# Attention and mixture-of-depths on one core: v's split parts stored once, by batch and chunk of 18 tokens, and fetched by an indirect gather

## The chip, the cores and the metric

The kernel runs on one core of a Trainium2 chip, as a single launch. The metric is the device time of that core in microseconds; the time given is the median of three executions, and one further execution was taken with the hardware profiler. Five engines work side by side, each through its own instructions in a fixed order: PE (matrix products), DVE (vector work), ACT (scalar functions), POOL and SP. SP and POOL also start the transfers (DMAs) between the device memory and the on-chip memory.

## What is computed

There are 8 batches, 8 heads, 576 tokens, head size 64 and 32 memory slots. Softmax weights of phi compress k and v into 32 memory slots for each head, each query attends to those slots, and a mixture-of-depths layer then adds a gated feed-forward result to the 128 tokens of highest score in each batch.

```
a = exp(phi - max(phi));  a = a / (sum(a) + 1e-9)          # over the 32 slots
k_m = einsum('bhsm,bhsd->bhmd', a, k)
v_m = einsum('bhsm,bhsd->bhmd', a, v)
scores = (q @ k_m^T) / 8;  attn = softmax(scores)
x = (attn @ v_m) as (batch, token, 8*64)
s = x @ w_gate;  top = the 128 tokens of largest s in each batch
out = x;  out[top] = x[top] + sigmoid(s[top]) * (relu(x[top] @ w1) @ w2)
```

## The kernel before

**Softmax.** The 8 heads of a batch are two groups of 4, so there are 16 pairs (batch, group). `chain_of` is the softmax of one pair on a tile of 128 partitions x 576 tokens. It is a chain of about twenty DVE passes (L332 to L401) and some ACT passes, and two chains run interleaved. `keys` then turns the result with PE transposes (L425), splits it into a high and a low part on ACT (`ahi`, L433) and DVE (`alo`, L435), sums k_m, and sends both parts to device memory as `a_lanes` (`store_a`, L474).

**Splitting v.** `split_v` loads v of a pair, `split` rounds it to a high part on ACT (L501) and takes the rest on DVE (L503), and `store_v` (L484) writes both parts to device memory as `v_lanes`. Each part is written twice, once for each value of `alpha`, since the products need high and low parts of a against high and low parts of v.

**The sum over tokens.** `sums` computes v_m token by token. Four batches (lanes) of 32 partitions each run at once, shifted against one another by LAG chunks. A chunk is T = 16 tokens and takes T x 4 = 64 matmuls (L564). There are 99 chunks. For each chunk `load_rows` fetches one tile of v (`load_v`, L521, one DMA over up to 128 partitions) and eight small tiles of a (`load_a`, L526) into one of three pairs of buffers (`v_rows`, `a_rows`). The memory on the chip is filled with zeros once at the start by POOL (L259), since the a tiles are block-diagonal.

**Attention and feed-forward.** When a batch's 576 tokens are summed, `attention` and `ffn` for it follow on the same engines.

**What sets the order.** The program is written by generators, one for each stream of work, and the class `Plan` decides at build time which step comes next. Each `yield` names an engine, an estimated duration, the buffers that are needed and the size of a transfer. A step with engine "Q" goes to SP or POOL, whichever the plan has free first. The result is a fixed order on each engine: an instruction that waits holds back everything behind it on that engine. Eight transfers can be under way on POOL's queue and eight on SP's, since each issue waits for the one eight places before it.

Of the kernel before, what the change touches and what calls it, by code (L numbers as in the profile page):

```python
# [8 lines left out]
F32 = mybir.dt.float32  # L9
# [3 lines left out]
I32 = mybir.dt.int32  # L13
I16 = mybir.dt.int16
AF = mybir.ActivationFunctionType
ALU = mybir.AluOpType
# [3 lines left out]
P = 128  # L20
# [12 lines left out]
RCP_B, RCP_S, RCP_C = 0.391, 0.70169533, 0.29830515  # L33
GRID, Y0, DH = 2.0 ** -11, 2.0 ** 14, 2.0 ** 9
Y0_BIAS = 14 * 0.6931471805599453
LANES, T, LAG, AHEAD = 4, 16, 9, 9


class Plan:
# [100 lines left out]
def kernel(  # L140
# [7 lines left out]
    w1: bass.AP,  # L148
    w2: bass.AP,
    out: bass.AP,  # L150
    v_lanes: bass.AP,
    a_lanes: bass.AP,
    capacity: int,
):
    nc = tc.nc
# [7 lines left out]
    H = NG * NPR  # L163
# [7 lines left out]
    per = S // T  # L171
    steps = (B - 1) * LAG + per
    assert LANES * LAG >= per
    assert capacity <= P and capacity < S and S % T == 0

    mem = ctx.enter_context(tc.tile_pool(name="mem", bufs=1))
    psum = ctx.enter_context(tc.tile_pool(name="psum", bufs=1, space=PSUM))
# [1 line left out]
    def sb(shape, dtype=F32, name="sb"):  # L179
        return mem.tile(list(shape), dtype, name=name)  # L180

    def several(n, shape, dtype=F32, name="sb"):
        return [sb(shape, dtype, f"{name}{i}") for i in range(n)]
# [11 lines left out]
    means = sb([P, NPR, P], name="means")  # L195
    ones16 = sb([P, P], BF16, name="ones16")
    ones = sb([P, 1], name="ones")
    good = sb([P, B], name="good")
    tgs = several(B, [P, NT, 2], name="tg")
    accs = [psum.tile([P, 512], F32, name=f"acc{i}") for i in range(LANES)]  # L200
# [6 lines left out]
        "ph": several(4, [P, S], name="ph"),  # L207
        "w": several(8, [P, S], name="w"),
        "i": several(2, [P, 2, S], I16, name="i"),
        "big": several(5, [P, S * Dh * NPR // P], name="big"),  # L210
        "vt": ["one", "two"],
        "kb": several(1, [PT, NC, NPR * Dh], name="kb"),
        "aS": several(1, [P, NPR, NC, M], name="aS"),
# [36 lines left out]
    def constants():  # L250
        nc.gpsimd.memset(blocks, 0.0)
        nc.gpsimd.memset(means, 0.0)
        for r in range(NPR):
            p = slice(r * M, (r + 1) * M)
            nc.gpsimd.memset(blocks[p, p], 1.0 / M)
            nc.gpsimd.memset(means[p, r], 1.0 / M)
        for pair in rows:
            for t in pair:
                nc.gpsimd.memset(t.bitcast(F32), 0.0)  # L259
        yield "POOL", 14.0  # L260
        nc.vector.tensor_sub(centre_m, ident, blocks)
        yield "wait", ("a", 0)
        yield "SP", 0.6, (), 256
        nc.sync.dma_start(out=wg, in_=bass.AP(
            tensor=w_gate.tensor, offset=w_gate.offset,
            ap=[[0, P]] + [list(x) for x in w_gate.ap]))
        yield "POOL", 8.0
        nc.gpsimd.iota(iota_r, pattern=[[1, capacity]], base=0, channel_multiplier=0,
                       allow_small_or_imprecise_dtypes=True)
        nc.gpsimd.iota(place, pattern=[[P, NT]], base=0, channel_multiplier=1,  # L270
                       allow_small_or_imprecise_dtypes=True)
        nc.gpsimd.memset(later, 1.0)
        nc.gpsimd.affine_select(
            out=later, in_=later, compare_op=ALU.is_gt, fill=0.0, base=0,
            pattern=[[1, S]], channel_multiplier=-1)
        nc.gpsimd.memset(ones16, 1.0)
        nc.gpsimd.memset(ones, 1.0)
        for t in tgs:
            nc.gpsimd.memset(t, 0.0)
            nc.gpsimd.iota(t[:, :, 0], pattern=[[P, NT]], base=0, channel_multiplier=1,  # L280
                           allow_small_or_imprecise_dtypes=True)
        for t in zs:
            nc.gpsimd.memset(t, 0.0)
            for r in range(NPR):
                nc.gpsimd.memset(t[r * M:(r + 1) * M, :, NPR * Dh + r:NPR * Dh + r + 1], 1.0)
        for t in rds:
            nc.gpsimd.memset(t, 1.0)
        signal("constants")
# [178 lines left out]
    def col(b):  # L467
        return start(b) * T
# [8 lines left out]
        signal(("a", b), 2 * NG)  # L477

    def store_v(b, g, w, src):
        yield "POOL", 1.4, (), 1152  # L480
        for alpha in range(2):
            r0 = ((b % LANES) * 4 + alpha * 2 + w) * H + g * NPR
            dst = v_lanes[r0:r0 + NPR, col(b):col(b) + S]
            nc.gpsimd.dma_start(out=dst.rearrange("h (j s) d -> j h (s d)", j=P // NPR), in_=src)  # L484
        put("big", src)
        signal(("v", b), 2 * NG)

# [20 lines left out]
    def lane(j, g):  # L508
        for b in range(g, B, LANES):
            if 0 <= j - start(b) < per:  # L510
                return b, j - start(b)

    def active(j):
        return [g for g in range(LANES) if lane(j, g)]

    turn = {}

    def load_v(j, eng):
        on = active(j)
        p = slice(32 * on[0], 32 * on[-1] + 32)  # L520
        eng.dma_start(out=turn[j][0].bitcast(F32)[p, :T], in_=v_lanes[p, j * T:(j + 1) * T])  # L521

    def load_a(j, h, eng):
        on = active(j)
# [7 lines left out]
    def load_rows():  # L532
        for j in range(steps):
            on = active(j)
            for g in on:
                b, n = lane(j, g)
                if n == 0:
                    yield "wait", ("v", b)
                    yield "wait", ("a", b)
            q, turn[j] = yield "Q", 0.65, ("rows",), 8 * T * (on[-1] + 1 - on[0])  # L540
            load_v(j, queues[q])
            signal(("rows", j), H + 1)
            for h in range(H):
                q, = yield "Q", 0.6, (), T * (on[-1] + 1 - on[0]) // 2
                load_a(j, h, queues[q])
                signal(("rows", j), H + 1)
# [375 lines left out]
```

## Time and profile before

| | us |
|---|---|
| median of three executions | 734.48 |
| lowest and highest of them | 728.63 and 737.57 |
| the profiled execution, its own time | 731.21 |
| span in its trace, first to last instruction | 729.5 |
| PE busy | 515.3 |
| DVE busy | 445.7 |
| POOL busy | 333.1 |
| ACT busy | 291.7 |

The busy times are sums over the whole span, and the program has stages that are limited by different things, so the table alone doesn't tell what a change in one stage is worth. 165.92 MB were moved, at 227 GB/s on average.

### The profile page before, as it was taken

To read this page: it belongs to the slowest core of one execution; us is meant where nothing else is said; L and a number is where in the kernel's file an instruction comes from. 1 tells how busy PE (TensorE), PEld (TensorE's weight loads), DVE (VectorE), ACT (ScalarE), POOL (GpSimd) and SP (SyncE) were. 2 spreads that over 40 slices of the span, in tenths; PEclk is the share of its full clock that TensorE was granted. 3 is DMA by queue.
4 is the path that set the end of the run, shared out by engine and by line. 5 is a ranking of instruction groups with operands and counts; after the bars stand their busy time and mean duration, and the time that the engine had idled before them with its cause. 6 is when DMAs were issued, how large, how long until landed. Compare 5 with 4: busy or idle time off the path is not lost. (4 is left out here: it accounts for less than half of the span.)

```text
span 729.5 us, 21974 instructions
## 1 busy us (share of the span) xinstructions
PE 515.3 (71%) x8754; PEld 418.8 (57%) x8754; DVE 445.7 (61%) x947; ACT 291.7 (40%) x721; POOL 333.1 (46%) x618
## 2 busy tenths in 40 slices
PE   0021572575776736766787896999999999989991
PEld 0010562465665735555666775678877887747760
DVE  8999987566764999967995222434353342547600
ACT  5466562441532746734663122322222322335310
POOL 9325763656555634554334544365566553010110
PEclk9985686787676757878779899899999999989997
DMA  4999699798889999999999799598865743141200
GB/s 162 384 358 343 168 299 286 201 251 208 215 226 255 362 356 258 318 342 365 284 282 332 235 295 347 179 291 230 226 176 142 175 117 101 37 138 37 66 30 19
DMA packets 74757, 165.92 MB, mean 227 GB/s; under 512 B 22296, under 2 KB 30488, under 8 KB 74648
## 3 DMA queue, kind: packets, MB, share of 16 engines
q0 software_dynamic: 32672, 88.23, 37.6%
q1 hardware_dynamic: 41976, 76.21, 35.5%
q8 instruction: 72, 1.18, 0.7%
q14 instruction: 37, 0.30, 0.1%
HBM read 96.21 MB, written 68.16 MB: 225 GB/s over the span
## 5 line engine op out<-in xcount | busy, mean ns | idle before, releaser
L564 PE MATMUL acc<-a_rows,v_rows 32*128 32x256 f32 x6336 | 253.0, 313 | 93.9 <-DMA a_rows<-a_lanes 63.3
L564 PEld LDWEIGHTS acc<-a_rows,v_rows 32*128 32x128 f32 x6336 | 231.7, 214 | 120.4 <-issue 61.3
L526 POOL DMA_DIRECT2D a_rows<-a_lanes x366 | 186.0, 514 | 122.8 <-PE acc L564 28.0
L706 ACT ACTIVATE w<-bank,rd 128x64 f32<-128x64 f32 (+1 forms) x320 | 69.4, 328 | 84.9 <-DVE rd L701 65.3
L824 PE MATMUL bank<-w,w 128*128 128x128 f32 x512 | 71.5, 292 | 1.0 <-ACT w L813 1.0
L824 PEld LDWEIGHTS bank<-w,w 128*128 128x128 f32 x512 | 65.3, 201 | 9.6 <-issue 4.2
L521 POOL DMA_DIRECT2D v_rows<-v_lanes x52 | 28.3, 545 | 87.3 <-PE acc L564 67.5
L840 PE MATMUL bank<-w,w 128*128 128x512 f32 x128 | 66.1, 622 | 0.0
L425 PE MATMUL bank<-ident,ph 128*96 128x128 f32 x96 | 21.8, 359 | 50.6 <-DVE ph L401 50.6
L693 PE MATMUL bank<-z,w 128*128 128x260 f32 (+1 forms) x160 | 49.2, 436 | 11.4 <-ACT w L654 10.3
L710 DVE TENSOR_TENSOR w<-w,hb 128x512 f32<-128x512 f32 (+1 forms) x40 | 27.5, 688 | 44.6 <-ACT w L706 43.4
L484 POOL DMA_DIRECT2D v_lanes<-big x64 | 35.4, 557 | 33.8 <-ACT big L501 13.3
L246 ACT ACTIVATE w<-i,c 128x576 f32<-128x576 int16 (+1 forms) x48 | 36.4, 766 | 26.1 <-DVE w L362 26.1
L429 ACT ACTIVATE aS<-bank 96x384 f32<-96x384 f32 x32 | 15.4, 486 | 77.2 <-PE bank L425 77.2
L425 PEld LDWEIGHTS bank<-ident,ph 128*96 128x96 f32 x96 | 14.3, 190 | 55.5 <-issue 44.8
L693 PEld LDWEIGHTS bank<-z,w 128*128 128x128 f32 (+1 forms) x160 | 28.7, 199 | 24.2 <-ACT w L654 11.6
L701 DVE RECIPROCAL rd<-bank 128x4 f32<-128x4 f32 (+1 forms) x80 | 11.8, 171 | 45.2 <-PE bank L693 44.9
L435 DVE TENSOR_TENSOR alo<-aS,ahi 96x768 f32<-96x768 f32 x16 | 15.2, 948 | 37.2 <-ACT ahi L433 37.0
L752 DVE SCALAR_TENSOR_TENSOR more<-w,tg,later 128x576 bf16<-128x576 f32 (+4 forms) x40 | 19.7, 546 | 23.9 <-ACT w L742 23.8
L713 DVE TENSOR_TENSOR w<-w,wg 128x512 f32<-128x512 f32 (+1 forms) x40 | 27.4, 686 | 10.4 <-PE bank L693 7.8
L802 POOL DMA_INDIRECT w<-out,idx x8 | 8.9, 1116 | 53.4 <-DVE idx L782 34.9
L474 POOL DMA_DIRECT2D a_lanes<-ahi x32 | 23.1, 724 | 21.8 <-ACT ahi L433 16.5
(118 smaller groups left out, 782.5 us busy)
## 6 DMA issues: line engine op xcount, KB each, us to landing
v_lanes<-big POOLq DMA_DIRECT2D x64, 576.0 KB
v_rows<-v_lanes SPq DMA_DIRECT2D x26, 512.0 KB
v_rows<-v_lanes POOLq DMA_DIRECT2D x19, 512.0 KB
big<-in_v SPq DMA_DIRECT2D x16, 576.0 KB
kb<-in_k SPq DMA_DIRECT2D x16, 576.0 KB
a_lanes<-ahi POOLq DMA_DIRECT2D x32, 288.0 KB
a_lanes<-alo POOLq DMA_DIRECT2D x32, 288.0 KB
big<-in_qT SPq DMA_DIRECT2D x16, 512.0 KB
```

What stands on the lines that cost most here:

```text
L246: nc.scalar.activation(dst, src, func, bias=biases[c] if c else 0.0, scale=s)
L425: nc.tensor.transpose(out=tp[:, c], in_=a[:, c0 + c], identity=ident)
L484: nc.gpsimd.dma_start(out=dst.rearrange("h (j s) d -> j h (s d)", j=P // NPR), in_=src)
L521: eng.dma_start(out=turn[j][0].bitcast(F32)[p, :T], in_=v_lanes[p, j * T:(j + 1) * T])
L526: eng.dma_start(out=turn[j][1].bitcast(F32)[32 * g0 + h:32 * g1:H, h].rearrange("p s m -> p (s m)"), in_=a_lanes[h, 4 * g0:4 * g1, j * T:( ...
L564: nc.tensor.matmul(out=accs[g][:, x * H * M:(x + 1) * H * M].rearrange("p (h m) -> p h m", m=M), lhsT=vr[p, s:s + 2].rearrange("p t d -> p ...
L693: nc.tensor.matmul(out=os[g][:n, :NPR * Dh + NPR], lhsT=e[:, g, t0:t0 + n], rhs=z[:, g], start=True, stop=True)
L706: nc.scalar.activation(x[:n, h * Dh:(h + 1) * Dh], os[g][:n, r * Dh:(r + 1) * Dh], AF.Copy, scale=rd[:n, c, h:h + 1])
L710: nc.vector.tensor_add(x[:n, :D], x[:n, :D], hb[:n].rearrange("p g r d -> p (g r d)"))
L713: nc.vector.tensor_mul(prod[:n, :D], x[:n, :D], wg[:n])
L824: nc.tensor.matmul(out=bank[:, f * P:f * P + n], lhsT=w1s[d, f0 // 4][:, f * P:(f + 1) * P], rhs=xeT[:, d * P:d * P + n], start=(d == 0), ...
L840: nc.tensor.matmul(out=bank[:n], lhsT=hT[f // 4][:, f % 4 * P:f % 4 * P + n], rhs=w2s[f], start=(f == 0), stop=(f == KF - 1))
```

## The change

The two parts of v are stored once. The new tensor `v_rows` in device memory is ordered by batch, chunk and row (16 rows, a part and a head each), and a row holds the 18 tokens of one chunk, 4,608 bytes. So `store_v` issues one DMA where it issued two. T becomes 18, and LAG and AHEAD become 8; a batch has 32 chunks, and there are 88 chunks in all. A chunk still covers 4 lanes, with 72 matmuls. `load_v` becomes an indirect DMA on POOL: for each of up to 128 partitions a row number is read from the on-chip table `v_row`, so that the 16 rows of a batch are each fetched to two partitions. The table is made in `constants()` at the start: POOL clears it and fills it with 32 iotas and one more (`lane_row`), and DVE takes a remainder and adds the two. The zero-filled buffers grow by the two tokens, and the pool `big` has 4 buffers in place of 5. The v load of each chunk is now planned on POOL alone, at 1.15 us; the a loads still go to SP or POOL.

```diff
-LANES, T, LAG, AHEAD = 4, 16, 9, 9
+LANES, T, LAG, AHEAD = 4, 18, 8, 8
...
+    v_row = sb([P, steps], I32, name="v_row")
+    lane_row = sb([P, 1], I32, name="lane_row")
...
-        "big": several(5, [P, S * Dh * NPR // P], name="big"),
+        "big": several(4, [P, S * Dh * NPR // P], name="big"),
...
             for t in pair:
                 nc.gpsimd.memset(t.bitcast(F32), 0.0)
+        nc.gpsimd.memset(v_row, 0)
+        for j in range(0, steps, LAG):
+            for g in active(j):
+                (b, n), g0 = lane(j, g), g - active(j)[0]
+                nc.gpsimd.iota(v_row[32 * g0:32 * g0 + 32, j:j + LAG], pattern=[[2 * H, LAG]],
+                               base=2 * H * (b * per + n), channel_multiplier=0)
+        nc.gpsimd.iota(lane_row, pattern=[[0, 1]], base=0, channel_multiplier=1)
         yield "POOL", 14.0
         nc.vector.tensor_sub(centre_m, ident, blocks)
+        nc.vector.tensor_single_scalar(lane_row, lane_row, 2 * H - 1, op=ALU.bitwise_and)
+        tt(out=v_row, in0=v_row, in1=lane_row.to_broadcast([P, steps]), op=ALU.add)
...
     def store_v(b, g, w, src):
-        yield "POOL", 1.4, (), 1152
-        for alpha in range(2):
-            r0 = ((b % LANES) * 4 + alpha * 2 + w) * H + g * NPR
-            dst = v_lanes[r0:r0 + NPR, col(b):col(b) + S]
-            nc.gpsimd.dma_start(out=dst.rearrange("h (j s) d -> j h (s d)", j=P // NPR), in_=src)
+        yield "POOL", 0.8, (), 576
+        r0 = w * H + g * NPR
+        nc.gpsimd.dma_start(out=v_rows[b, :, r0:r0 + NPR], in_=src)
...
-    def load_v(j, eng):
+    def load_v(j):
         on = active(j)
         p = slice(32 * on[0], 32 * on[-1] + 32)
-        eng.dma_start(out=turn[j][0].bitcast(F32)[p, :T], in_=v_lanes[p, j * T:(j + 1) * T])
+        nc.gpsimd.indirect_dma_start(
+            out=turn[j][0].bitcast(F32)[p, :T].rearrange("p t d -> p (t d)"), out_offset=None,
+            in_=v_rows[:max(lane(j, g)[0] for g in on) + 1].rearrange("b n r x -> (b n r) x"),
+            in_offset=bass.IndirectOffsetOnAxis(ap=v_row[:p.stop - p.start, j:j + 1], axis=0))
...
-            q, turn[j] = yield "Q", 0.65, ("rows",), 8 * T * (on[-1] + 1 - on[0])
-            load_v(j, queues[q])
+            turn[j], = yield "POOL", 1.15, ("rows",), 8 * T * (on[-1] + 1 - on[0])
+            load_v(j)
```

The first place is the head of DVE's order, up to the first maximum and subtraction of the softmax chains. Before, it reads as follows; the words in brackets are the semaphores that the instruction waits for (POOL's own, a DMA queue's, DVE's own).

```order
L261 TENSOR_TENSOR centre_m<-ident,blocks 128x128 [waits Pool_49]
L332 TENSOR_REDUCE sm_160<-ph_116 128x1 [waits DMAHW0_49]
L335 TENSOR_SCALAR ph_116<-ph_116,sm_160 128x576 [waits DVE_49]
L332 TENSOR_REDUCE sm_161<-ph_117 128x1 [waits DMAHW1_49]
L335 TENSOR_SCALAR ph_117<-ph_117,sm_161 128x576 [waits DVE_49]
```

After, the same place reads:

```order
L270 TENSOR_TENSOR centre_m<-ident,blocks 128x128 [waits Pool_49]
L271 TENSOR_SCALAR lane_row<-lane_row 128x1 [waits Pool_49]
L272 ISA v_row<-lane_row,v_row 128x176 [waits DVE_49]
L343 TENSOR_REDUCE sm_161<-ph_118 128x1 [waits DMAHW0_49]
L346 TENSOR_SCALAR ph_118<-ph_118,sm_161 128x576 [waits DVE_49]
L343 TENSOR_REDUCE sm_162<-ph_119 128x1 [waits DMAHW1_49]
L346 TENSOR_SCALAR ph_119<-ph_119,sm_162 128x576 [waits DVE_49]
```

Two instructions for the row table have come in ahead of every softmax instruction, and the first of them waits for POOL.

The second place is what that wait is for: POOL's order from the last zero fill to the first stores of v, here before.

```order
L259 MEMSET v_rows_110 128x1088
L259 MEMSET a_rows_111 128x4096
L484 DMA v_lanes<-big_132 32x4x1152 x2
L484 DMA v_lanes<-big_130 32x4x1152 x2
L484 DMA v_lanes<-big_133 32x4x1152 x2
```

After, it reads:

```order
L261 MEMSET v_rows_112 128x1216
L261 MEMSET a_rows_113 128x4608
L262 MEMSET v_row 128x88
L266 IOTA v_row 32x8 x32
L268 IOTA lane_row 128x1
L493 DMA v_rows<-big_134 32x4x1152
L493 DMA v_rows<-big_132 32x4x1152
```

The table's 34 instructions stand behind the six zero fills, and `lane_row`, for which DVE waits, is the last of them. Each part of v is stored by one DMA in place of two.

The third place is POOL's order around the stores of a for batch 1's second group, when v of the third and later batches is being stored (a number behind a name is a buffer's). Before:

```order
L484 DMA v_lanes<-big_131 32x4x1152 x2
L484 DMA v_lanes<-big_132 32x4x1152 x2
L484 DMA v_lanes<-big_133 32x4x1152 x2
L484 DMA v_lanes<-big_134 32x4x1152 x2
L474 DMA a_lanes<-ahi_138 96x4x192 x2
L474 DMA a_lanes<-alo_140 96x4x192 x2
L521 DMA v_rows_106<-v_lanes 64x1024
L526 DMA a_rows_107<-a_lanes 8x512 x4
```

After:

```order
L493 DMA v_rows<-big_132 32x4x1152
L493 DMA v_rows<-big_133 32x4x1152
L538 DMA a_rows_113<-a_lanes 4x576
L530 DMA v_rows_108<-v_rows,v_row 32x1152
L538 DMA a_rows_109<-a_lanes 4x576 x3
L493 DMA v_rows<-big_134 32x4x1152
L493 DMA v_rows<-big_135 32x4x1152
L530 DMA v_rows_110<-v_rows,v_row 32x1152
L485 DMA a_lanes<-ahi_139 96x4x192 x2
L485 DMA a_lanes<-alo_141 96x4x192 x2
L538 DMA a_rows_111<-a_lanes 4x576 x2
L530 DMA v_rows_112<-v_rows,v_row 64x1152
```

Eight stores of v in a row have become four, spread out between row loads, ahead of the same four stores of a.

## Rows read from the trace of the kernel before

**Rows 1.** Busy time by stretch: PE, PEld, DVE, ACT, POOL; PE clock, DMA share, GB/s.

```profile
0.00:376.00 376.00, 198.77 (x4030) 173.13 (x4034) 307.62 (x545) 191.94 (x340) 197.41 (x376) 0.76 0.91 282
376.00:404.00 28.00, 21.61 (x419) 18.25 (x411) 17.15 (x43) 10.19 (x42) 12.84 (x22) 0.97 0.97 323
404.00:716.00 312.00, 294.92 (x4313) 227.41 (x4313) 120.95 (x363) 89.58 (x340) 122.84 (x221) 0.97 0.55 162
```

**Rows 2.** DVE's waits up to 376 us: us in total, times, longest.

```profile
DVE alo L435 <- ACT ahi L433: 37.0, 5, 10.4
DVE ph L341 <- ACT i L246: 11.2, 2, 10.9
```

**Rows 3.** DVE in order of time, its start and the last softmax pass: start, us.

```profile
3.94 0.75 DVE L332 TENSOR_REDUCE sm<-ph 128x1 f32<-128x576 f32 x1 [0.62 <-DMA ph<-in_phiT]
4.73 3.24 DVE L335 TENSOR_SCALAR ph<-ph,sm 128x576 f32<-128x576 f32 x1
7.89 0.73 DVE L332 TENSOR_REDUCE sm<-ph 128x1 f32<-128x576 f32 x1
...
375.03 0.82 DVE L401 SCALAR_TENSOR_TENSOR ph<-ph,sm,i 128x576 f32<-128x576 f32 x1
```

**Rows 4.** POOL in order of time: a zero fill and the first stores of v.

```profile
4.14 3.52 POOL L259 MEMSET a_rows<- 128x4096 f32 x1
...
17.02 4.58 POOL L484 DMA_DIRECT2D v_lanes<-big  x8
```

**Rows 5.** POOL's groups of instructions: busy us, mean ns of one, idle before.

```profile
L526 POOL DMA_DIRECT2D a_rows<-a_lanes x366 | 186.0, 514 | 122.8 <-PE acc L564 28.0 <-DMA a_rows<-a_lanes 21.8 <-DMA a_lanes<-alo 17.7
L484 POOL DMA_DIRECT2D v_lanes<-big x64 | 35.4, 557 | 33.8 <-ACT big L501 13.3 <-DVE big L503 7.7 <-DMA v_rows<-v_lanes 3.6
L521 POOL DMA_DIRECT2D v_rows<-v_lanes x52 | 28.3, 545 | 87.3 <-PE acc L564 67.5 <-issue 6.2 <-PE bank L693 5.5
...
L259 POOL MEMSET a_rows<- 128x4096 f32 x3 | 10.8, 3615 | 0.0
...
L802 POOL DMA_INDIRECT w<-out,idx x8 | 8.9, 1116 | 53.4 <-DVE idx L782 34.9 <-ACT gr L784 13.1 <-DMA out<-w,idx 2.1
L259 POOL MEMSET v_rows<- 128x1088 f32 x3 | 3.3, 1108 | 0.1
L280 POOL IOTA tg<- 128x5 f32 x8 | 1.1, 138 | 0.6
```

**Rows 6.** POOL's v loads of line 521: ns, shortest, median and longest.

```profile
L521 POOL DMA_DIRECT2D v_rows<-v_lanes x52: 513/548/594, 73.2 to 611.0; - x52
```

**Rows 7.** POOL's indirect stores of line 849, in the same form.

```profile
L849 POOL DMA_INDIRECT out<-w,idx x8: 967/1046/1885, 436.6 to 715.1; - x8
```

**Rows 8.** DMA queues, POOL's own: packets, MB, share of 16 engines' span.

```profile
q0 software_dynamic: 32672, 88.23, 37.6%
```

**Rows 9.** POOL in order of time, 103 to 129 us; in brackets idle before, releaser.

```profile
103.75 3.33 POOL L484 DMA_DIRECT2D v_lanes<-big  x6 [1.20 <-DVE w L359]
...
112.00 0.68 POOL L474 DMA_DIRECT2D a_lanes<-alo  x1 [0.43 <-DMA v_lanes<-big]
...
124.27 4.42 POOL L526 DMA_DIRECT2D a_rows<-a_lanes  x8 [8.14 <-DMA a_lanes<-alo]
```

**Rows 10.** PE in order of time: the chunk that starts at 126 us.

```profile
126.30 3.79 PE L564 MATMUL acc<-a_rows,v_rows 32*128 32x256 f32 x64 [11.04 <-DMA a_rows<-a_lanes]
```

**Rows 11.** DVE in order of time, where it waited, 130 to 330 us.

```profile
132.99 0.95 DVE L435 TENSOR_TENSOR alo<-aS,ahi 96x768 f32<-96x768 f32 x1 [7.00 <-ACT ahi L433]
...
186.92 1.55 DVE L341 SCALAR_TENSOR_TENSOR ph<-i,ph 128x576 f32<-128x576 int16 x2 [10.91 <-ACT i L246]
...
324.67 0.95 DVE L435 TENSOR_TENSOR alo<-aS,ahi 96x768 f32<-96x768 f32 x1 [6.23 <-ACT ahi L433]
```

**Rows 12.** PE's waits from 404 us on, the longest first.

```profile
PE bank L693 <- ACT w L654: 5.8, 1, 5.8
```

**Rows 13.** ACT in order of time, 454 us.

```profile
454.88 0.66 ACT L654 ACTIVATE w<-bank 128x256 f32<-128x256 f32 x2 [10.60 <-DMA out<-w]
```

More of the change, by code (lines that the diff above doesn't have):

```diff
@@ L150 @@
     out: bass.AP,
-    v_lanes: bass.AP,
+    v_rows: bass.AP,
     a_lanes: bass.AP,
@@ L173 @@
     assert LANES * LAG >= per
-    assert capacity <= P and capacity < S and S % T == 0
+    assert capacity <= P and capacity < S and S % T == 0 and P // NPR == per and per % LAG == 0
     mem = ctx.enter_context(tc.tile_pool(name="mem", bufs=1))
@@ L915 @@
     cols = (B - 1) * LAG * T + S + 7
-    v_lanes = nc.dram_tensor("v_lanes", (LANES * 4 * H, cols, Dh), F32, kind="Internal").ap()
+    v_rows = nc.dram_tensor("v_rows", (B, S // T, 2 * H, T * Dh), F32, kind="Internal").ap()
     a_lanes = nc.dram_tensor("a_lanes", (H, LANES * 4, cols, M), F32, kind="Internal").ap()
     with tile.TileContext(nc) as tc:
-        kernel(tc, *args, out, v_lanes, a_lanes, int(moe_capacity))
+        kernel(tc, *args, out, v_rows, a_lanes, int(moe_capacity))
     r = run_bass_kernel_spmd(nc, [arrays], core_ids=[0])
```

## The prediction, made before the changed kernel had run

> **What bounds the kernel now.** I read the busy time by stretch first, then the waits of the engine that is fullest in each stretch, and last the order of time around those waits. Three stretches differ [rows 1]. Up to 376 us, where the last softmax pass starts [rows 3], DVE is busy for 307.6 us (82%), the DMA engines' share is 0.91, and PE is busy for just over half, at a granted clock of 0.76. From 404 us to the end PE is busy for 294.9 of 312 us at 0.97, and the DMA share is down to 0.55. So the kernel is DVE and transfers first and PE afterwards, and a transfer saved helps only where it ends a wait of DVE early or of PE late.
>
> What does DVE wait for in the first stretch? Nearly all of it is two kinds, 37.0 and 11.2 us, five and two times [rows 2], and both stand behind ACT, which stands behind PE: a transpose for the softmax lies on PE behind a chunk of the token sum, and the chunk lies behind its row loads. One instance in order: POOL issued six v stores from 103.75 us (two more just before), issued the last store of a at 112.00, and idled 8.14 us until that had landed before it went on with row loads at 124.27 [rows 9]; PE's chunk started at 126.30 after 11.04 us of idling [rows 10]; DVE had idled 7.00 us when it went on at 132.99 [rows 11]. So stores of v do cost DVE time, there.
>
> **The store halved.** 64 stores of v become 32. In bytes: 64 x 0.590 MB (a tile of 128 x 1,152 numbers) is 37.7 of the 88.23 MB on POOL's queue, whose packets take 37.6% of 729.5 us, 274 us [rows 8]. Half of v is 18.9 MB, 58.6 us of all 16 DMA engines at that queue's mean. Most of that isn't worth its length. While DVE is the fuller engine, only the waits shorten. Going through them:
> - The wait of 7.00 us at 133 us: eight stores ahead of it become four, and the store of a lands earlier. I take all 7 us back (bounds 0 and 11, PE's wait).
> - The four waits of that kind between 140 and 240 us, of which one stands in [rows 11] (10.91; the others are of 5.8 to 10.4 us): no v store is issued in that stretch, since 32 of the 64 [rows 5] come before 107 us and 32 from 245 us on. I take 0; fewer chunks (27 become 24 to the same token) might give up to 10 back, and the gathers, below, might take 12.
> - The wait of 6.23 us at 325 us [rows 11] lies among v stores again. I take 3 (bounds 0 and 6).
> - From 404 us on: PE's longest wait, 5.8 us [rows 12], is for ACT, which idled 10.60 us for a buffer whose store to the output hadn't landed [rows 13], behind eight stores of v. I take 4 (bounds 0 and 6).
>
> Together 14 us back, between 0 and 33.
>
> **The row table at the start.** This part adds a wait. DVE's first softmax pass started at 3.94 us [rows 3], as soon as phi had landed. In the new order `lane_row` and `v_row` stand ahead of it, and `lane_row` waits for the last of POOL's table instructions, which stand behind the zero fills. Before, POOL came to its first DMA at 17.02 us [rows 4]. The fills grow with their tiles: 10.8 us x 512/4096 is 1.35, and 3.3 us x 128/1088 is 0.39 [rows 5]. 33 iotas at 0.138 us each [rows 5] are 4.55 us, and the clear of the table some 0.15, by the same row. That makes 23.5 us; with the two small DVE passes, at some 0.2 us each by estimate from the iota's row, the first maximum starts near 23.8 us. What this costs isn't the 20 us between the starts: the pass behind that maximum took 3.24 us while POOL's fill of 4.14 to 7.66 us ran [rows 3, 4], and the second maximum came at 7.89. After, with no fill running, the second maximum comes some 1.3 us behind the first (0.75 and about half a us), at 25.1. So DVE is 17 us late from there. If an iota takes half the row, or twice it, the delay is 15 or 22 us. Everything of both chains is queued behind, on DVE and, through it, on ACT and PE. From 20 to 120 us nothing absorbs it: nearly all of DVE's waits in [rows 2] come after 125 us.
>
> **The gathers.** 88 on POOL at 1.116 us (the kernel's other indirect load, [rows 5]) are 98.2 us. They replace 52 v loads on POOL (28.3), 32 stores (half of 35.4) and 28 a loads that move to SP, where 47 v loads have gone (28 x 0.514 is 14.4; 366 become 338 by the new order). POOL's sum rises by 98.2 - 28.3 - 17.7 - 14.4 = 38 us. From 404 us on POOL is busy for 122.8 of 312 us [rows 1], and three buffer pairs let loads run ahead, so there I cost it at nothing. Before 240 us a row load is waited for; there each gather is 0.57 us longer than a plain load, 14 us for the 24 chunks if all of it shows. I take 0, since half of the load's issues stand on the other queue, and keep 0 to 12 (a v load on SP had gone beside POOL's). The longest indirect store took 1.885 us [rows 7]; with that for each gather, POOL's sum would rise by 106.
>
> The rest has one answer: the matmuls are the same 6,336, the DVE passes of the softmax are unchanged, SP loses 107 issues off the path, and one `big` less is met by buffers that come back after one DMA instead of two.
>
> A rule of the Trainium skill speaks against the gathers. POOL's 52 v loads took between 513 and 594 ns [rows 6], all through the softmax passes. The Trainium skill, SBUF — State Buffer, section SBUF: two separate sides, says that a DVE operation in a two-port mode locks GpSimd out, so that a DMA from its queue can't have its descriptors written. By that rule the loads now moved to POOL could each lie behind a subtraction of line 335, and with half a us for each of its 16 that would be 8 us more. The trace doesn't show it, and I add nothing.
>
> **The sum.** 17 late, less 7, 0, 3 and 4: 3 us. On the profiled execution that is 731.2 + 3 = 734. That execution lies 3.3 us under the median of the runs, so for the median I say 734.5 + 3, rounded down: **737 us**.
>
> **Rivals.**
> - *Faster: the transfers bound more than I allow.* For it speaks the share of 0.91 up to 376 us, and that the 37.0 and 11.2 us of DVE's waits hang on row loads. If half of them, 24 us, comes back in place of my 10, and PE's 4 and the 17 stay, and 12 more come from PE's stretch running without its other 13 us of idling, the sum is 17 - 24 - 4 - 12, some -20: 715. Against it: DVE's work alone, 304 us from a start at 23.8, ends at 328, so no more than 48 us can be won before 376 even with no wait left, and the waits from 140 to 240 us have no v store near.
> - *Slower: the wait at the start goes through whole.* The place is DVE's head, the price 17 us, and it decides if DVE's waits after 125 us don't shrink when DVE comes late to them, since each is for a chunk whose loads hang in turn on stores of a that DVE has made late. With nothing regained but PE's 2 or so, 734.5 + 17 is 751.
> - *Slower: the gather is longer than the small one shows.* It moves 4,608 bytes a row where the other moved 2,048. At 1.885 us, 24 chunks x 1.34 us is 32 us in the part up to 240 us, and the time is 734.5 + 3 + 32, near 769. Against it: the indirect load's mean lies much nearer to 1.1, and its number of rows is the same.
>
> **How the numbers follow.** Forecast 0.5, transfers 0.2, wait in full 0.2, slow gather 0.1. Two per cent, 15 us, is about what a measurement of this kernel can tell from no change, and it bounds the three cases: the forecast lies within, the first rival beyond on the fast side, the other two beyond on the slow side. The forecast's own bounds, 15 - 33 on one side and 22 + 12 on the other, would reach from 716 to 768 if every term fell the same way; I take 714 to 758, which holds both the first and second rival and leaves out the slow gather and a larger gain.
>
> **What would show it.** DVE's first maximum near 24 us, with POOL named as its releaser and the second some 1.3 us later; the last softmax pass starting between 375 and 392 us; the wait near 133 us gone or below 3 us; POOL's busy time near 375 us and the gathers near 1.1 us each; some 19 MB less on the queues; PE still busy for about 95% behind the softmax. I am wrong if the last softmax pass is well before 365 us, which would mean that transfers held the first stretch; if DVE's first maximum isn't late; or if PE waits for the gathers in the late stretch, where I cost them at nothing.

## The result, and the profile after

| | before | after |
|---|---|---|
| median | 733.1 us (19 executions) | 723.14 us (19 executions) |
| lowest and highest | 727.6 and 737.58 | 716.3 and 731.62 |
| ratio, 95% interval | | 0.9855 [0.9829, 0.988] |
| span of the profiled execution | 729.5 us | 717.9 us |

The changed kernel is faster by 1.45%, 10.6 us; forecast were 3 us slower. Below, a difference between two kernels is taken from their ratios to the kernel before, times 733.1 us, so that 1% is 7.3 us; each ratio is sure to about half a per cent, a difference to about 5 us. Disturbed executions are left out of the ratios but not of the medians, which matters for e9 (median 742.66 us, ratio 1.0023), and the profiles of e9 and e10 are of such executions.

Busy time by stretch after, which answers to [rows 1]:

```profile
0.00:376.00 376.00, 193.51 (x4201) 170.99 (x4201) 297.34 (x519) 187.24 (x333) 226.95 (x397) 0.85 0.80 244
376.00:404.00 28.00, 19.36 (x310) 15.41 (x313) 21.47 (x59) 13.68 (x49) 16.92 (x27) 0.77 0.99 298
404.00:716.00 312.00, 291.14 (x4252) 225.29 (x4244) 123.09 (x373) 90.30 (x341) 132.57 (x205) 0.98 0.51 150
```

Up to 376 us the DMA share fell from 0.91 to 0.80, and DVE got 10 us less done. PE's mean granted clock there rose from 0.76 to 0.85, and the same matmuls keep PE busy for 504 us in all, where it had been 515; no run separates this from loads that come sooner. DVE in order of time at its start, and its last softmax pass, answer to [rows 3]:

```profile
23.82 0.15 DVE L271 TENSOR_SCALAR lane_row<-lane_row 128x1 int32<-128x1 int32 x1 [20.51 <-POOL lane_row L268]
24.00 0.25 DVE L272 CUSTOM_DVE_ANT_0 v_row<-lane_row,v_row 128x176 uint16<-128x176 uint16 x1
24.17 0.75 DVE L343 TENSOR_REDUCE sm<-ph 128x1 f32<-128x576 f32 x1
24.95 0.52 DVE L346 TENSOR_SCALAR ph<-ph,sm 128x576 f32<-128x576 f32 x1
25.39 0.74 DVE L343 TENSOR_REDUCE sm<-ph 128x1 f32<-128x576 f32 x1
...
394.44 0.82 DVE L412 SCALAR_TENSOR_TENSOR ph<-ph,sm,i 128x576 f32<-128x576 f32 x1
```

The second maximum starts 17.5 us later than before, and the last pass 19.4 us later. Still, what stands behind the softmax ends 11.6 us earlier. DVE's waits between 120 and 240 us (us in total, times, longest), before:

```profile
DVE alo L435 <- ACT ahi L433: 30.8, 4, 10.4
DVE ph L341 <- ACT i L246: 10.9, 1, 10.9
```

After:

```profile
DVE alo L446 <- ACT ahi L444: 14.0, 3, 7.7
DVE ph L352 <- ACT i L248: 5.5, 2, 4.9
DVE alo L446 <- DMA a_rows<-a_lanes: 5.4, 1, 5.4
```

41.7 us of waiting became 24.9: 17 of them came back in the stretch in which I had taken 7. The wait that stood near 133 us is still there, at 4.42 us where it had 7.00:

```profile
150.60 0.95 DVE L446 TENSOR_TENSOR alo<-aS,ahi 96x768 f32<-96x768 f32 x1 [4.42 <-ACT ahi L444]
```

POOL's groups and POOL's queue after, for [rows 5] and [rows 8]:

```profile
L538 POOL DMA_DIRECT2D a_rows<-a_lanes x338 | 173.6, 522 | 63.0 <-DMA v_rows<-v_rows,v_row 26.7
L530 POOL DMA_INDIRECT v_rows<-v_rows,v_row x88 | 96.5, 1096 | 91.7 <-PE acc L576 45.4
...
L493 POOL DMA_DIRECT2D v_rows<-big x32 | 18.1, 568 | 36.1 <-ACT big L510 17.0
...
q0 software_dynamic: 31424, 88.75, 39.4%
```

The gathers are 1,096 ns each and POOL is busy for 376.4 us, both as forecast. POOL's queue carries no less than before: the v loads that SP's queue had (76.21 MB before, 56.80 after) took the place of the stores. PE's longest wait from 408 us on is now 1.2 us (in the row with the most, 2.9 us in all), where [rows 12] had 5.8:

```profile
PE acc L576 <- issue: 2.9, 5, 1.2
```

One view ranks the runs below nearly as their times do (e1 and e13 change places, and so do e3 and e11): the stretch from 480 us to the end, in which PE is busy almost without a break, so that PE's busy time there (the first after the length) is what the earlier stretches have left over. Before:

```profile
480.00:1000.00 520.00, 225.21 (x3298) 173.22 (x3294) 97.60 (x295) 70.95 (x277) 88.05 (x157) 0.98 0.21 60
```

After:

```profile
480.00:1000.00 520.00, 219.66 (x2959) 165.12 (x2957) 102.29 (x317) 73.62 (x287) 87.59 (x133) 0.99 0.18 51
```

### The profile page after: what moved, and what is told of

It is laid out like the page before. It is cut to its first block, busy times and chain, and to the rows that moved or that the text cites. A ratio compares the mean times of both kernels' runs of the same rounds, so it can differ in the third digit from the quotient of the medians.

```text
span 717.9 us, 21620 instructions
## 1 busy us (share of the span) xinstructions
PE 504.0 (70%) x8754; PEld 411.7 (57%) x8754; DVE 441.9 (62%) x949; ACT 291.2 (41%) x721; POOL 376.4 (52%) x628
## 3 DMA queue, kind: packets, MB, share of 16 engines
q1 hardware_dynamic: 35320, 56.80, 27.3%
## 4 chain that ended last, share of the span: by engine, by line
PE 39%; DMA 24%; DVE 14%; POOL 10%; issue 7%; SPq 3%; ACT 2%; DVEq 0%; POOLq 0%; ACTq 0%
PE acc L576 16%; DMA a_rows<-a_lanes 10%; PE bank L836 8%; PE bank L852 7%; DMA v_rows<-v_rows,v_row 6%; PE bank L705 3%; POOL a_rows L538 3%; SPq L538 3%; DMA big<-in_qT 2%; DMA a_lanes<-alo 2%; POOL v_rows L530 2%; POOL a_rows L261 2%; POOL a_lanes L485 1%; ACT w L718 1%; DVE big L512 1%
## 5 line engine op out<-in xcount | busy, mean ns | idle before, releaser
L576 PEld LDWEIGHTS acc<-a_rows,v_rows 32*128 32x128 f32 x6336 | 234.2, 216 | 119.7 <-issue 65.0
L538 POOL DMA_DIRECT2D a_rows<-a_lanes x338 | 173.6, 522 | 63.0 <-DMA v_rows<-v_rows,v_row 26.7
L530 POOL DMA_INDIRECT v_rows<-v_rows,v_row x88 | 96.5, 1096 | 91.7 <-PE acc L576 45.4
L836 PEld LDWEIGHTS bank<-w,w 128*128 128x128 f32 x512 | 62.7, 191 | 16.9 <-issue 10.9
L836 PE MATMUL bank<-w,w 128*128 128x128 f32 x512 | 67.7, 280 | 2.5 <-ACT w L825 1.6
L705 PE MATMUL bank<-z,w 128*128 128x260 f32 (+1 forms) x160 | 45.7, 408 | 1.5 <-DVE less L781 0.9
L857 DVE SCALAR_TENSOR_TENSOR w<-bank,gr,w 128x512 f32<-128x512 f32 x8 | 6.0, 750 | 55.1 <-PE bank L852 30.4
L493 POOL DMA_DIRECT2D v_rows<-big x32 | 18.1, 568 | 36.1 <-ACT big L510 17.0
L861 POOL DMA_INDIRECT out<-w,idx x8 | 8.3, 1036 | 49.6 <-DVE w L857 36.3
L248 ACT ACTIVATE i<-ph 128x576 int16<-128x576 f32 x32 | 21.6, 677 | 28.1 <-DVE ph L346 27.3
```

Source lines behind the costliest of these rows:

```text
L248: nc.scalar.activation(dst, src, func, bias=biases[c] if c else 0.0, scale=s)
L493: nc.gpsimd.dma_start(out=v_rows[b, :, r0:r0 + NPR], in_=src)
L530: nc.gpsimd.indirect_dma_start(out=turn[j][0].bitcast(F32)[p, :T].rearrange("p t d -> p (t d)"), out_offset=None, in_=v_rows[:max(lane(j, ...
L538: eng.dma_start(out=turn[j][1].bitcast(F32)[32 * g0 + h:32 * g1:H, h].rearrange("p s m -> p (s m)"), in_=a_lanes[h, 4 * g0:4 * g1, j * T:( ...
L576: nc.tensor.matmul(out=accs[g][:, x * H * M:(x + 1) * H * M].rearrange("p (h m) -> p h m", m=M), lhsT=vr[p, s:s + 2].rearrange("p t d -> p ...
L705: nc.tensor.matmul(out=os[g][:n, :NPR * Dh + NPR], lhsT=e[:, g, t0:t0 + n], rhs=z[:, g], start=True, stop=True)
```

## The experiments

The first four took the change apart into three theories. A: the gain is the halved stores in the late stretch, and the wait at the head is made up for by 240 us. B: the gain is the coarser chunk and the order that the plan makes for it. C: the wait goes through whole and the rest is worth 27 us.

**e1. The table late.** The changed kernel, with DVE's two passes over the table moved behind most of the softmax of the first two pairs (they start at 46.0 us, and the first maximum is back at 3.72):

```
+        yield "wait", ("half", 0, 1)
         nc.vector.tensor_single_scalar(lane_row, lane_row, 2 * H - 1, op=ALU.bitwise_and)
```

> The changed kernel with its two DVE passes for the row table moved behind the softmax of the first pair; nothing else moves on any engine. Theory A (the wait at the head of DVE is absorbed by 240 us, since the token sum's row loads pace PE and DVE there): DVE's first maximum is back near 4 to 8 us, but the whole time falls by 0 to 4 us against the changed kernel, to 719 to 723. Theory C (the wait goes through, and the rest of the change is worth 27 us): the time falls by 12 to 17 us, to 706 to 711.

Measured: 714.84 us, ratio 0.9761 [0.9708, 0.9814]. The wait costs 0.94%, 7 us, in the changed kernel: less than half of its 17.5.

**e2. The wait alone.** The kernel before with the table's 34 POOL instructions and 2 DVE passes, whose result nothing reads:

```
+        nc.gpsimd.memset(v_row, 0)
+        for i in range(32):
+            nc.gpsimd.iota(v_row[...], pattern=[[2 * H, 8]], base=i, channel_multiplier=0)
...
+        tt(out=v_row, in0=v_row, in1=lane_row.to_broadcast([P, 88]), op=ALU.add)
```

> The kernel before with nothing added but the row table's 34 POOL instructions and the two DVE passes that wait for them (the table is used by nothing). Theory A: DVE's first maximum near 24 us, and the whole time 0 to 5 us above the kernel before, 733 to 738. Theory C: the time rises by 14 to 17 us, to 747 to 750.

Measured: 743.63 us, ratio 1.0139 [1.0079, 1.0199]: 10 us. With e1, the wait's price is 7 to 10 us, each sure to about 5; that lies between the forecasts of A and C in both runs, so C falls, and so does A's "made up for".

**e3. Second stores.** The changed kernel, each part of v stored a second time, to a tensor that nothing reads:

```
         nc.gpsimd.dma_start(out=v_rows[b, :, r0:r0 + NPR], in_=src)
+        nc.gpsimd.dma_start(out=v_more[b, :, r0:r0 + NPR], in_=src)
```

> The changed kernel with each part of v stored a second time, to a tensor that nothing reads, so that 64 stores go out as in the kernel before; the order is otherwise the same. Theory A (the gain is the halved stores, above all those near 440 us that held back the output's stores and with them ACT and PE): the time rises by 8 to 14 us against the changed kernel, to 731 to 737, and PE's busy share from 404 us on falls again. Theory B (the gain is the coarser chunk and the order that the plan makes of it): it rises by 0 to 4 us, to 723 to 727.

Measured: 750.88 us, ratio 1.0266 [1.022, 1.0312]. In this fixed order the halved stores are worth 4.1%, 30 us, over twice what A had for them; e1 and e15 (below), the same pair with the table late, give 28.5. Two thirds of that stand before the softmax ends: the last pass starts 20 us later than the changed kernel's 394.44:

```profile
414.49 0.82 DVE L413 SCALAR_TENSOR_TENSOR ph<-ph,sm,i 128x576 f32<-128x576 f32 x1
```

The rest shows later, in e3's busy time by stretch (from 400 to 480 us the DMA share is 0.97, and from 480 us on PE has 241 us left):

```profile
400.00:480.00 80.00, 70.21 (x1166) 58.69 (x1167) 36.22 (x104) 25.87 (x88) 47.49 (x77) 0.87 0.97 318
...
480.00:1000.00 520.00, 241.02 (x3384) 183.12 (x3383) 105.23 (x322) 75.10 (x291) 104.36 (x160) 0.98 0.21 62
```

DVE's waits between 120 and 240 us, of which the changed kernel has 24.9 us, are little longer, 28.7:

```profile
DVE ph L353 <- ACT i L249: 20.3, 2, 13.2
DVE alo L447 <- ACT ahi L445: 7.4, 3, 3.9
DVE ph L397 <- ACT w L249: 1.0, 1, 1.0
```

**e4. Chunks of 18 alone.** The kernel before, with its two stores, its plain v loads on either queue and no table:

```
-LANES, T, LAG, AHEAD = 4, 16, 9, 9
+LANES, T, LAG, AHEAD = 4, 18, 8, 8
...
-        "big": several(5, [P, S * Dh * NPR // P], name="big"),
+        "big": several(4, [P, S * Dh * NPR // P], name="big"),
```

> The kernel before with chunks of 18 tokens, LAG and AHEAD 8 and four big buffers, but with v stored twice and loaded by plain DMAs on either queue, no table. Theory A: 730 to 736, as the kernel before. Theory B: 715 to 723, below the changed kernel since there is no wait at the start.

Measured: 706.04 us, ratio 0.9637 [0.9593, 0.9681], the best so far. Chunks of 18 are worth 3.6%, 26.6 us; the rest of the change, halved stores and all, loses 16 of them. Between 120 and 240 us DVE waits for 28.7 us, as in e3; the longest:

```profile
DVE ph L341 <- ACT i L246: 12.8, 3, 8.2
DVE ph L399 <- ACT i L396: 6.1, 2, 3.3
DVE alo L435 <- ACT ahi L433: 4.6, 2, 2.5
```

So most of the 17 us that the change wins in that stretch go with the coarser chunk, with every store still there. PE has 207 us left from 480 us on:

```profile
480.00:1000.00 520.00, 206.67 (x3004) 159.80 (x2996) 89.48 (x276) 66.14 (x255) 71.42 (x126) 0.99 0.18 51
```

So two things were open: what in chunks of 18 gains so much, and what in the rest costs 46 us beside a gain of 30.

**e7. Chunks of 12.** One line, `LANES, T, LAG, AHEAD = 4, 12, 12, 12`, in the kernel before.

> The kernel before with chunks of 12 tokens (132 chunk steps for 99; 88 with chunks of 18), nothing else changed. Theory B1 (each chunk step has a price, about 2.4 us by the run with chunks of 18: 26 us for 11 steps): 733 plus 33 x 2.4, about 800 or more. Theory B2 (the new order, which the plan makes for chunks of 18, happened to be a better one, steps as such are nearly free): 715 to 760.

Measured: 795.1 us, ratio 1.085 [1.0801, 1.0899]: 62 us for 33 steps, 1.9 each; 26.6 us for 11 steps in e4 is 2.4 each. Both ways the time goes with the number of steps, which speaks against one lucky order.

**e9. Four tiles for v's parts**, the other line of e4's diff alone.

> The kernel before with four tiles for v's parts where it has five, chunks of 16 as before. Theory B1 (the gain of chunks of 18 is the price of 11 chunk steps): the tile changes little or harms, 728 to 745. Theory B3 (the fewer tiles, and the order the plan makes for them, are what gained 26 us in the run with chunks of 18): 705 to 718.

Measured: ratio 1.0023 [0.9938, 1.0108]. With chunks of 16 the tile makes no difference that shows, and nothing near 26.6 us.

**e16. More loads of a, same steps.** e4, with every second load of a (one for each of 8 heads and step) cut into two by partitions:

```
+        half = (g1 - g0) * 2
+        for u in ([slice(0, half), slice(half, 2 * half)] if h % 2 == 0 else [slice(0, 2 * half)]):
...
```

> The kernel with chunks of 18 alone (706 us), every second load of a cut into two loads of half the partitions each, on the same queue at the same place: 88 steps, the same bytes and rows, and 1,056 loads of a (as with chunks of 12, which took 795 us) in place of 704; PE, DVE and ACT keep their order. Theory R1 (the price of a step is its loads as such): 770 to 795. Theory R2 (it is the step itself: its buffer, its waits, its place in the order): 700 to 725.

Measured: 778.26 us, ratio 1.07 [1.0644, 1.0756]: 78 us for 352 loads, 0.22 us each, with not a byte of a more. From e4 to e7 it is 352 loads of a and 44 of v, and 89 us: 0.22 us each again. So the loads of a step account for its price. Busy time from 120 to 240 us (columns as in [rows 1]) of e4:

```profile
120.00:240.00 120.00, 74.07 (x1785) 67.44 (x1789) 88.36 (x149) 53.22 (x85) 64.46 (x118) 0.82 0.93 256
```

The same of e16:

```profile
120.00:240.00 120.00, 72.77 (x1546) 65.50 (x1546) 72.72 (x133) 42.33 (x68) 75.29 (x139) 0.72 0.79 218
```

POOL's busy time rises, DVE's falls by 16 us, and the DMA share falls from 0.93 to 0.79. So it isn't bandwidth that runs short there; the loads come out of the queues more slowly. What one load's price is made of was not tried. The lengths of the issues come near it (ns, shortest, median and longest, of all loads of a in e16):

```profile
L528 SPq DMA_DIRECT2D a_rows<-a_lanes x544: 471/568/2899, 60.3 to 650.3; - x182
L528 POOL DMA_DIRECT2D a_rows<-a_lanes x512: 483/521/818, 69.3 to 649.3; - x171
```

At the medians, SP's 173 loads more and POOL's 179 are 98 and 93 us of issuing, side by side, against 78 measured; the profile doesn't count SP's as busy time. The eight transfers that may be under way on a queue are another rival: a cut load takes two of the eight places. And the halves have half the partitions of the loads that they replace, which e7's have not.

**e6. Plain v loads in the gathers' places.** Chunks of 18, two stores, no table, each chunk's v by one plain load on POOL. To get the changed kernel's order, the plan is told the changed kernel's numbers, for the stores too:

```
-        yield "POOL", 1.4, (), 1152
+        yield "POOL", 0.8, (), 576
...
-            q, turn[j] = yield "Q", 0.65, ("rows",), 8 * T * (on[-1] + 1 - on[0])
-            load_v(j, queues[q])
+            turn[j], = yield "POOL", 1.15, ("rows",), 8 * T * (on[-1] + 1 - on[0])
+            load_v(j, nc.gpsimd)
```

> Chunks of 18, v's parts stored twice in two places, no table, and each chunk's v fetched by one plain load on POOL in the gather's place: every engine's order is that of the run with second stores (751 us), but for the table and the kind of the load. Theory D1 (the gather instruction itself is what is slow): 706 to 722. Theory D2 (the place in POOL's queue, all v loads behind all stores, is what costs): 738 to 750, that is 751 less the 4 to 10 us of the table's wait.

Measured: 735.84 us, ratio 1.0036 [1.0006, 1.0066]. That lies between the forecasts, 2 us from D2's: 29 us of e4's gain go with no gather at all, by v loads that are POOL's and the order that the plan makes for them and for its new price of a store.

**e13 and e14. Queue or order.** Each keeps one order of all instructions and changes only the queue of v loads: e13 is e4 with SP's v loads issued by POOL in place, e14 is e6 with every second one issued by SP.

```
-            load_v(j, queues[q])
+            load_v(j, nc.gpsimd)
```

```
-            load_v(j, nc.gpsimd)
+            load_v(j, (nc.sync, nc.gpsimd)[j % 2])
```

> The kernel with chunks of 18 alone (706 us), its 40 to 46 v loads that SP issued now issued by POOL at the same place; every other instruction keeps engine and order. Theory N1 (POOL's queue, its 45 more issues and its waits, is what costs): 728 to 740. Theory N2 (the plan's other order is what costs): 702 to 714.

> The kernel with plain v loads all in POOL's order (736 us), every second one issued by SP in its place; every other instruction keeps engine and order. Theory N1 (POOL's queue): 706 to 718. Theory N2 (the plan's order): 730 to 742.

Measured:

| | v loads shared by both queues | all on POOL |
|---|---|---|
| e4's order | 0.9637 (e4) | 0.9822 [0.9772, 0.9872] (e13, 717.04 us) |
| e6's order | 1.0008 [0.9965, 1.0051] (e14, 733.02 us) | 1.0036 (e6) |

The order costs 27 or 16 us, down either column; the queue 13.6 us in the one order and nothing measurable in the other. e13 lies between the forecasts of N1 and N2, e14 where N2 had it. So neither theory holds alone: N2 is the larger part, and from e4 to e6 by way of e13 it is 13.6 for the queue and 15.7 for the order. POOL's queue carries 107.68 MB in e13 and 88.50 in e4. Where the order costs: up to 480 us PE's waits for loads of a are, in e13,

```profile
PE acc L564 <- DMA a_rows<-a_lanes: 74.0, 24, 9.3
```

and in e6,

```profile
PE acc L564 <- DMA a_rows<-a_lanes: 101.1, 28, 16.3
```

**e15. The gather itself.** e3 with e1's line: e6's order but for the table's instructions and gathers.

> The run with gathers and second stores (751 us) with DVE's two passes over the table moved behind the first token scores, as in the run with the late table; every other instruction keeps engine and order. Its order is then that of the run with plain loads on POOL (736 us), but for the table's instructions and the gathers. Theory P1 (the 15 us between the two are the table's wait): 735 to 741. Theory P2 (the gather itself costs 5 to 12 us, the wait the rest): 741 to 748.

Measured: 742.92 us, ratio 1.015 [1.0086, 1.0214]. From e6, the gathers, with the table's instructions that come with them, cost 8.4 us (P2); to e3, the wait costs 8.5, as in e1 and e2. The v loads of e6, in ns, shortest, median and longest:

```profile
L521 POOL DMA_DIRECT2D v_rows<-v_lanes x88: 507/542/597, 70.6 to 592.7; - x88
```

The gathers of e15, in the same form:

```profile
L533 POOL DMA_INDIRECT v_rows<-v_rows,v_row x88: 882/990/1497, 76.3 to 600.2; - x88
```

**e8, e10, e11. Why the stores cost.** e8 cuts each store of the changed kernel in two by partitions (same bytes, 32 more instructions); e10 issues its stores from SP in place; e11 is e3 with the second stores from SP.

```
+        for u in range(2):
+            nc.gpsimd.dma_start(out=v_rows[b, u * per // 2:(u + 1) * per // 2, r0:r0 + NPR],
+                                in_=src[u * P // 2:(u + 1) * P // 2])
```

```
-        nc.gpsimd.dma_start(out=v_rows[b, :, r0:r0 + NPR], in_=src)
+        nc.sync.dma_start(out=v_rows[b, :, r0:r0 + NPR], in_=src)
```

> The changed kernel with each v store cut into two stores of half the partitions: the same bytes, 32 more DMA instructions in POOL's queue, all else in the same order. Theory H1 (the second stores of the run with 751 us cost by their bytes): 721 to 727. Theory H2 (they cost by their instructions in POOL's queue, ahead of gathers): 740 to 752.

> The changed kernel with v's 32 stores issued by SP where POOL issued them, at the same place in the program's order; every other instruction keeps its engine and order. Theory K (what sets the pace is the bytes in POOL's own transfer queue: 107 MB cost some 28 us more than 88 MB, whether the 19 MB were second stores or v loads moved there from SP): 18.9 MB less in that queue gives 695 to 712. Theory L (all bytes count alike, whatever their queue): 718 to 726. Theory M (SP, which now waits for ACT and DVE at 32 places with loads behind them, delays these): 730 or more.

> The run with second stores (751 us), the second store of each part issued by SP in place of POOL. Theory K (bytes in POOL's queue): 723 to 735, near the changed kernel. Theory L (all bytes alike): 745 to 755. Theory M (waits in SP's order): above 755.

Measured: e8 728.29 us, 0.9959 [0.992, 0.9997], 7.6 us or 0.24 us for each store more; e10 717.03 us, 0.9792 [0.9736, 0.9848], 4.6 us better than the changed kernel, hardly clear of the noise; e11 751.19 us, 1.0243 [1.0183, 1.0303], no different from e3. So second stores cost the same on either queue: theory K (bytes in POOL's queue) falls for them, and L holds; e10 lies just below L's 718, and its 4.6 us are a small part of what K wanted. If a second store costs by its instruction what e8's halves do, some 8 of the 30 us are the 32 instructions, and 22 are left for the 18.9 MB.

**e5. Rows named twice by plain loads.** The changed kernel without gathers and table; each chunk's v by one plain load for each lane, with a repeated dimension:

```
+        src = bass.AP(tensor=row.tensor, offset=row.offset, ap=[[0, 2], [T * Dh, 2 * H], [1, T * Dh]])
...
+        eng.dma_start(out=dst.rearrange("p t d -> p (t d)"), in_=src)
```

> The changed kernel without the gather and without the table: v's parts are stored once, and each chunk's v is fetched by one plain load for each of its lanes (2 to 4) whose address pattern names the rows twice; SP and POOL share these loads as the plan deals them out. Theory D (the gather itself and its place in POOL's queue cost what chunks of 18 gain; halved stores help in any case): at or below the kernel with chunks of 18 alone, 706 us, down to 680. Theory E (the halved stores only help where POOL's queue is loaded with gathers, 751 to 723): 700 to 712. Theory G (many more loads cost more than the stores save): above 715.

Measured: 954.15 us, ratio 1.3026 [1.2969, 1.3082], theory G beyond its size. 168 more loads at 0.22 us would be 37 us; these loads are slow themselves. From 480 to 590 us, at a DMA share of 0.65, e5's loads of v, of 144 KB each, took from issue to landing (us, shortest, median and longest, of those whose landing the trace has):

```profile
DMA to landing us min/median/max: 7.8/8.9/11.2
```

In the same stretch of e4, at a share of 0.63, these loads were of 144 to 432 KB:

```profile
DMA to landing us min/median/max: 2.7/4.3/5.0
```

SP's issues of loads of a waited for them to land, in e5 for 170 us in all:

```profile
SPq L526 <- DMA v_rows<-v_rows: 170.2, 74, 5.2
```

In e4 it is 16:

```profile
SPq L526 <- DMA v_rows<-v_lanes: 16.0, 15, 3.5
```

Since the loads themselves are slow, the run tells nothing on the worth of halved stores. What in the form of the load is slow wasn't tried; the repeat of 2 is its outermost dimension, and no other order of the dimensions was run.

**e12. The pieces that gain, together.** e1 with v's stores dealt out by the plan:

```
-        yield "POOL", 0.8, (), 576
+        q, = yield "Q", 0.8, (), 576
...
-        nc.gpsimd.dma_start(out=v_rows[b, :, r0:r0 + NPR], in_=src)
+        queues[q].dma_start(out=v_rows[b, :, r0:r0 + NPR], in_=src)
```

> The changed kernel with its table late (715 us) and v's stores dealt out between SP and POOL by the plan as the other transfers are, with the new order that this makes. Theory K: 690 to 706, faster than the kernel with chunks of 18 alone. Theory L: 711 to 719. Theory M: above 720.

Measured: 698.04 us, ratio 0.9545 [0.9502, 0.9588], faster than both kernels (3.1% under the changed one) and than e4 by 0.9%, 7 us. From e1 it is 16 us. That is where K had it (690 to 706) and not L, but K's reason failed in e10, where the queue itself gave 4.6 us; so the other order that the plan makes is probably the larger part again, which no run with that order fixed shows. From 480 us on PE has 200 us left:

```profile
480.00:1000.00 520.00, 199.59 (x2638) 151.35 (x2633) 89.98 (x279) 66.16 (x256) 75.76 (x114) 0.99 0.15 43
```

## Why the prediction was wrong

The runs give a sum in place of mine, term by term, in us at 733.1:

| step | runs | forecast | measured |
|---|---|---|---|
| chunks of 18 | before to e4 | 0 (up to 10 back) | -26.6 |
| v loads all in POOL's queue | e4 to e13 | 0 | +13.6 |
| the order that goes with it | e13 to e6 | 0 | +15.7 |
| gathers in place of plain loads | e6 to e15 | 0 (0 to 12) | +8.4 |
| the table's wait | e15 to e3 | +17 | +8.5 |
| stores halved | e3 to after | -14 (0 to 33 back) | -30.1 |
| sum | | +3 | -10.5 |

The sizes hold along this row of kernels; by e14 the second and third would be 2 and 27. That the forecast of 737 lies only 14 us off is luck: the six errors are -26.6, 13.6, 15.7, 8.4, -8.5 and -16.1.

**The step that failed** is the one in which "fewer chunks" was taken as 0. I counted the loads that leave POOL (366 become 338) and read them as moved to SP; that "SP loses 107 issues", 47 loads of v and 60 of a, I put down as off the path. In fact 792 loads of a, 8 for each of 99 steps, became 704, and with 11 v loads less that is 99 loads. At e16's 0.22 us each they are 22 of the 26.6 us. A load was costed by its issue on an engine that isn't full, which made it free; in e16 each had a price, with all else kept. The Trainium skill, DMA: Bandwidth & Descriptors, section Rules for kernel authors, says to coalesce many small transfers, since under 64 KB one pays mostly overhead. The loads of a are of 9 to 36 KB, and e16, with its 0.22 us a load and not a byte of a more, agrees. The 64 KB aren't borne out as a bound: e8's halves are of 288 KB and cost 0.24 us each. The rule would have put a gain of the coarser chunk into the sum, though not its size.

**The stores** were mis-sized: the direction was right, and I had 14 of 30 us. I priced only the transfers that stood ahead of four named waits, with 10 us up to 376 us and 4 behind. Without the second stores the softmax ends 20 us earlier (394.44 against e3's 414.49), and 10 more come behind it. The 17 us of waits that went between 120 and 240 us are mostly not the stores': e3 and e4, which store everything twice, have 28.7 us there. So my 0 for the stores between 140 and 240 us was about right. Which waits hold the stores' other 16 us stays open. By e8 some 22 of the 30 are bytes, and e11 has the same price on either queue. The rival of transfers that bound more comes nearer than the forecast, at 715 (its own terms, 17 - 24 - 4 - 12, make -23 and 711). That is luck as well: it had no chunk in it, and no cost of gathers to set against.

**The gathers at nothing** was wrong too, by 37.7 us in three parts, of which the instruction is the smallest. I looked at POOL's busy time, which came out right (376.4 us), and at the length of one gather (1,096 ns), right as well. What I left out is that v loads which either queue could take became POOL's alone, and that the plan's order of everything follows. What in that order is dear stays open: it differs on every engine, and PE's waits for loads of a up to 480 us grow with it from 74.0 to 101.1 us. The rule of the Trainium skill that I set aside there (SBUF — State Buffer, section SBUF: two separate sides: a DVE operation in a two-port mode holds up descriptors written for GpSimd's queue) still isn't seen: with all 88 v loads on POOL in e6 the longest took 597 ns, against 594 for the 52 before [rows 6].

**The wait** was right in place and length: 24.17 us for the first maximum (23.8 forecast), 17.5 us late at the second (17). Of the 17.5, 7 to 10 are left at the end. The rival in which it goes through whole (751) is refuted by e1, e2 and e15, which agree on 7 to 10 us.

Of what I listed as signs, POOL's time, the gathers, the 18.9 MB and the head were right, and so was PE's share behind the softmax (285 of 296 us from 408 us on). The wait near 133 us came out at 4.42 us, above my 3. The last softmax pass came at 394.4, past my 392, and yet the end was early. So that sign was a bad one: DVE being late at 394 us says little when less token sum is left for PE behind it. In e4, too, that pass starts later than before (383.27 against 375.03), and e4 is 26.6 us faster.

## What to carry to other kernels

Count the transfers, not only their bytes and the busy time of the engine that issues them: here each small load cost 0.22 us of the whole kernel, and the tile size that gave fewer of them was worth nearly as much (26.6 us) as the halved stores that the change was built around (30.1). Add up the issues on SP as well as on POOL, since the busy time doesn't hold SP's. Where a planner sets the order, an edit that ties an operation to one queue also buys a new order; keep that apart by swapping the queue alone in a fixed order, as e13 and e14 do. A change of several parts can gain by one and lose by the others: taking them apart led to a kernel (e12, the table late and the stores on either queue) that is 3.1% faster than the change as it was made.

## What the runs showed of the hardware

A plain load of 144 KB with its rows named twice by a repeated dimension landed in 7.8 to 11.2 us, where plain loads of 144 to 432 KB took 2.7 to 5.0 at nearly the same DMA share (e5 and e4, 480 to 590 us). In e5 POOL's queue had far more packets than in e4 for fewer bytes: 56,272 for 70.05 MB, against 31,024 for 88.50. They are small ones: on all queues the packets under 512 B are 49,406 in e5 and 20,848 in e4, those of 512 B and more 46,318 and 50,412. POOL's queue in e5 (packets, MB, share):

```profile
q0 software_dynamic: 56272, 70.05, 25.9%
```

In e4:

```profile
q0 software_dynamic: 31024, 88.50, 38.9%
```

On e16's queues, POOL's 179 loads more (512, in e4 333) brought 5,728 packets more, 32 each, all under 512 B by the page's counts (26,576, in e4 20,848); SP's 173 loads more brought none. Both queues in e16:

```profile
q0 software_dynamic: 36752, 88.53, 36.8%
q1 hardware_dynamic: 40128, 75.93, 32.1%
```
